# A layer norm with a spectral filter and an MLP: residual and bias on VectorE, W2 in SyncE's queue, the first square root on ScalarE, and a new order

## The chip, the cores and the metric

The kernel runs on one core of a Trainium2 chip. The metric is the device time of one execution in microseconds. Profiles are of one execution each; all times of instructions are counted from the start of its span.

## What is computed

```python
def reference(A_x, A_w_r, A_w_i, B_x, B_w1, B_b1, B_w2, B_b2):
    def _A_ref(x, w_r, w_i):              # x is (1, 2048, 640)
        X = rfft2(x.astype(float32)); X = X * (w_r + 1j * w_i)
        return irfft2(X, s=(S, D)).astype(bfloat16)
    def _B_ref(x, w1, b1, w2, b2):        # w1 is 640 x 1536, w2 is 1536 x 640
        h = gelu(einsum("bsd,df->bsf", x, w1) + b1)
        return einsum("bsf,fd->bsd", h, w2) + b2
    xn = _layernorm(A_x)                  # over the 640 columns, eps 1e-5
    return A_x + _A_ref(xn, A_w_r, A_w_i) + _B_ref(xn, B_w1, B_b1, B_w2, B_b2)
```

All inputs and the output are bf16.

## The kernel before

The 2048 rows are cut into 16 tiles of 128 rows, tile c holding the rows 16p + c. Both branches start from the same normalized tiles, and their results meet in PSUM.

**Normalization** (L574 to L603). For each tile VectorE takes statistics of two halves (`bn_stats`), aggregates them to mean and variance, adds eps (`ve`), GpSimd raises this to -1/2 (`rstd`, L580), VectorE forms `nmr = -mean * rstd` (L582) and then `x * rstd + nmr` (L603) into a buffer `xn`, of which there are two (for one pair of tiles each). Transposed tiles `xnT` come from PE (L619) with a copy by VectorE or ScalarE, or for the tiles in `BYDMA` from a DMA transpose that SyncE issues (L608).

**The spectral branch.** For each pair of tiles VectorE forms sums and differences (L632, L636), PE multiplies with the table `gtab` ("aps"), the result lies in `XV`. Then come six groups of products with `etab` (b0 to b5), evacuated to `Xb`; small 32 x 32 products with `mtab` (c00 to c31, first digit P of four steps, two each), evacuated to `Y`; the filter on VectorE, four products `T = Y * Wf` (L737) and four sums `Z` (L741) for each step P; small products with `ntab` (d00 to d31), evacuated to `U`; 16 DMA transposes of U into `XV` (L762); six groups with `getab`, evacuated to `Wf`, sums on VectorE (L788, L793), and last a product with `htab` into the output's PSUM.

**The MLP branch.** The W1 products ("hps") run in six blocks of 1, 1, 2, 4, 4 and 4 tiles, each for 12 pieces of 128 hidden columns; ScalarE applies Gelu (L670) into `gT`. The W2 products are 12 pairs of 512 and 128 columns for a tile. For tiles in `KEEP` they are done early and emptied to SBUF with b2 added (L839); for the others they are accumulated in the same PSUM as the `htab` product. VectorE's final add (L850) joins PSUM and the kept part, and SyncE stores the tile.

**Residual and b2.** For each tile there is an f32 place of 640 columns (`xo`), in `xnT` for tiles in `HOME`, else in `X`. It first holds b2 (a copy by ScalarE, L818) or the kept W2 result plus b2 (L839); then GpSimd issues a DMA that adds x from HBM to it (L841, accumulating). `QUIET` says for which transfers this DMA has to wait.

**What sets the order.** Every operation is given to `Sched` with an engine, a cost, a priority and its operands. `schedule` walks through time: of the operations that can start within 0.03 us of the earliest, the one with the highest priority is put next in its engine's queue; `sync` then places semaphore waits. So queues are fixed when the kernel is built, and an engine waits at an operation whose operands are late, with everything behind it. PSUM has eight banks, `ZONE` says which group may use which of them; `CHAIN` fixes the sequence of the b, c and d groups on PE, so that they alternate with MLP products. `WARM` gives the number of products on zeros with which PE starts (54, and 6 more behind the first transposes).

**Loads.** SyncE issues x, b1, most of W1, `gtab` and the 34 strided parts of the filter `Wf`, each with its own semaphore; ScalarE issues the identity and W1's first part; GpSimd issues `etab`, `mtab`, b2, W2 in four parts, `ntab`, `getab`, `htab`. W1 comes in parts of 2, 3 and 7 pieces of 128 columns.

Of the kernel before, what the change touches and what calls it, by code (L numbers as in the profile page):

```python
# [84 lines left out]

SWITCH = 0.095
HOLD = 0.04


def mm_us(n):  # L90
    return max(n / 2400.0 + 0.0027, 0.0265)
# [65 lines left out]
class Sched:  # L157
# [6 lines left out]
    def op(self, engs, prio, emit, reads=(), writes=(), after=(), nbytes=0, gate=(), rate=330e3, alts=None, late=0.0):  # L164
        o = Op()
        o.name = writes[0].name if writes else ""
        o.engs, o.prio, o.emit = engs, prio, emit
# [26 lines left out]
    def schedule(self):  # L194
# [24 lines left out]
        while left:  # L219
# [47 lines left out]
            if o.nbytes:  # L267
                if e == "pool":
                    dma_free = max(t + 2.0, dma_free) + o.nbytes / o.rate
                    o.end = max(t + 4.6, dma_free + 1.2)  # L270
                else:
                    s = max(t + 1.3, dma_free)
                    dma_free = s + o.nbytes / o.rate
                    o.end = dma_free + 0.35
            else:
                o.end = t + dur + LAT[e]
# [96 lines left out]
W1P = ((0, 2), (2, 5), (5, 12))  # L373
GROUPS = [(0, 2), (2, 3), (5, 3), (8, 3), (11, 3), (14, 2)]
BYDMA = (4, 8, 9, 10, 12, 14, 15)
WLATE = (17.0, 1.08)
ANY = [(0, 8)]
ZONE = {'hps': [(4, 8)], 'bps': [(0, 4)], 'cps': [(0, 4)], 'dps': [(0, 4)], 'eps': [(0, 4), (4, 8)], 'fin': [(4, 8), (0, 4)], 'fps': [(4, 8)], 'tps': [(0, 8)], 'aps': [(0, 8)]}
PRIO = {'hps': -60.2, 'gelu': -255.2, 'pb': 147.1, 'pc': 112.6, 'filt': 344.6, 'ipc': 182.7, 'eps': 72.7, 'fin': 71.9}
AHEAD = 1  # L380
EARLY = 4
CHAIN = "b0 b1 c00 c01 b2 c10 d01 c11 d00 b4 b3 c20 d10 c21 d11 b5 d20 d21 c30 c31 d31 d30".split()
XASPLIT = [((0, 1, 2, 3, 4),)] * 7 + [((0, 1), (2, 3, 4))]
KEEP = (0, 3, 5, 6, 7, 8, 11, 12, 14)
HOME = (0, 3, 1, 2, 4, 9, 10, 13)
QUIET = {0: 1, 3: 0, 6: 4, 9: 4, 12: 0, 15: 0, 1: 0, 2: 2, 4: 4, 5: 0, 7: 0, 8: 0, 10: 3, 11: 0, 13: 3, 14: 3}
WARM = (54, 6)
# [3 lines left out]
def bass_parallel_sum__spectral_gfnet__dense_activation_gelu__prompt_kernel(  # L391
# [21 lines left out]
    with ExitStack() as es:  # L413
# [22 lines left out]
        first = sb("first", [128, 1])  # L436
# [5 lines left out]
        nmr = sb("nmr", [128, 16], F32)  # L442
# [14 lines left out]
        XN, X1, XF = 0, 4 * D, 6 * D  # L457
# [7 lines left out]
        p_xn, p_x1, p_xf, p_xb, p_y, p_t, p_z, p_u = Pool(2), Pool(1), Pool(2), Pool(2), Pool(2), Pool(2), Pool(2), Pool(3)  # L465
# [25 lines left out]
        B_mh, B_xbpad, B_wpad, B_warm = Buf("mhalf"), Buf("xbpad"), Buf("wpad"), Buf("warm")  # L491
        K.op([("dve", 0.1)], 300, lambda e, _: e.memset(warm[:], 0.0), writes=[B_warm])
        K.op([("pool", 0.1)], 100, lambda e, _: e.memset(mhalf[:], -0.5), writes=[B_mh])
# [4 lines left out]
        K.op([("act", 1.45)], 300, lambda e, _: e.activation(first[:], warm[:, 0:1], ACT.Gelu_apprx_tanh), reads=[B_warm])  # L498
# [10 lines left out]
        B_g, B_e, B_m, B_n, B_ge, B_h, B_w2 = [Buf(x) for x in ("g", "e", "m", "n", "i", "h", "w2")]  # L509
# [15 lines left out]
        load_w1(1)  # L525
        load_x(2, 2)
        for j in range(2, len(W1P)):
            load_w1(j)
# [4 lines left out]
        for dst, src, buf, nbytes, rate, late in (  # L533
                (etab[:], const["E"], B_e, 204800, 250e3, 18.0), (mtab[:], const["M"], B_m, 65536, 130e3, 21.0),
                (b2bc[:], bass.AP(tensor=b2v.tensor, offset=b2v.offset, ap=[[0, 128], [1, D]]), B_b2b, 163840, 395e3, 22.0),
                *[(W2[:, 3 * j:3 * j + 3, :], w2v[:, 3 * j:3 * j + 3, :], B_w2, 3 * 128 * D * 2, 330e3, 24.0 + 4.0 * j) for j in range(4)],
                (ntab[:], const["N"], B_n, 49152, 130e3, 40.0), (getab[:], const["GE"], B_ge, 204800, 250e3, 50.0),
                (htab[:].rearrange("p a b -> p (a b)"), const["H"], B_h, 524288, 330e3, 55.0)):
            load(dst, src, buf, nbytes, rate=rate, q="pool", after=x_in, late=late)
        WP = 32 * KP  # L540
# [19 lines left out]
        pe([("128", 0.1)], 200, lambda: [(psb(B_b1ps.slot, [[1, NFC]]), b1t[:], ident[0:NFC, 0:NFC], True, True)], reads=[B_b1, B_id], writes=[B_b1ps])  # L560
        K.op([("act", 0.2)], 200, lambda e, _: e.activation(b1col[:], psb(B_b1ps.slot, [[1, NFC]]), ACT.Copy), reads=[B_b1ps], writes=[B_b1c])

# [5 lines left out]
        for c0, n in [(0, 1), (1, 1)] + [(c, 2) for c in range(2, 16, 2)]:  # L568
            pr = 100 - c0 / 2
            B_mv, B_ve, B_r = Buf("mv"), Buf("ve"), Buf("r")  # L570
            for c in range(c0, c0 + n):
                B_st = Buf("st")
                for h in range(2):
                    K.op([("dve", 0.393)], pr, lambda e, _, c=c, h=h: e.bn_stats(stats[:, c, 6 * h:6 * h + 6], view(X, c * D + H2 * h, [[1, H2]])),  # L574
                         reads=[B_x[c]], writes=[B_st], gate=first_ve if c == 1 else [])
                K.op([("dve", 0.119)], pr, lambda e, _, c=c: e.bn_aggr(mv[:, c, :], stats[:, c, :]), reads=[B_st], writes=[B_mv])
            a, b = c0, c0 + n
            o = K.op([("dve", 0.09)], pr, lambda e, _, a=a, b=b: e.tensor_scalar_add(ve[:, a:b], mv[:, a:b, 1], 1e-5), reads=[B_mv], writes=[B_ve])  # L578
            first_ve = first_ve or [o]
            K.op([("pool", 0.65)], pr, lambda e, _, a=a, b=b: e.tensor_tensor(out=rstd[:, a:b], in0=ve[:, a:b], in1=mhalf[:, a:b], op=ALU.pow),  # L580
                 reads=[B_ve, B_mh], writes=[B_r])
            K.op([("dve", 0.071)], pr, lambda e, _, a=a, b=b: e.scalar_tensor_tensor(out=nmr[:, a:b], in0=mv[:, a:b, 0], scalar=-1.0,  # L582
                                                                                     in1=rstd[:, a:b], op0=ALU.mult, op1=ALU.mult),
# [303 lines left out]
```

## Time and profile before

| | us |
|---|---|
| five runs, median (lowest to highest) | 152.91 (151.93 to 153.45) |
| the profiled execution | 151.77 |
| its span, first to last instruction | 149.6 |
| busy in the span: PE / VectorE / ScalarE / GpSimd | 143.1 / 110.7 / 79.5 / 33.0 |
| PE's first product on data, end of its last | 7.71, 147.19 |
| granted TensorE clock | 1.00 |

Busy time by stage (us), from the windows view:

| stage | from, to | PE | VectorE | ScalarE |
|---|---|---|---|---|
| head, until the first W1 product | 0, 7.71 | 6.47 | 3.27 | 2.16 |
| first tiles | 7.71, 13.69 | 5.82 | 5.91 | 5.11 |
| normalization, W1 blocks 0 to 2 | 13.69, 28.30 | 14.56 | 14.52 | 12.48 |
| normalization, W1 block 3 | 28.30, 46.70 | 18.29 | 16.26 | 15.79 |
| b0 to the first d group | 46.70, 62.83 | 15.35 | 10.71 | 7.56 |
| to the first getab group | 62.83, 110.95 | 46.85 | 28.96 | 29.63 |
| to PE's last product | 110.95, 147.19 | 35.71 | 30.76 | 6.74 |

How to read the profile's lines: an engine's line gives start, length, engine, line of the kernel, operation, out<-in with shapes, and in brackets how long the engine had been idle and who released it. A line of the waits view reads: engine and what it did, `<-` whom it waited for, us in total, times, the longest. A line of the groups view ends in busy us, the mean ns of one, and the idle time ahead of it. SPq, DVEq and so on are the engines' sequencers, which issue DMAs and process waits. Matmuls overlap in the records, so that lengths of single ones are longer than their distance; a few matmul records are missing.

### The profile page before, as it was taken

How to read it: one execution, taken by the hardware profiler on the slowest of the kernel's cores; microseconds unless marked ns; L12 is line 12 of the kernel's file. 1: busy time of each engine (PE TensorE's matmuls, PEld its weight loads, DVE VectorE, ACT ScalarE, POOL GpSimd, SP SyncE). 2: the span in 40 equal slices, each digit the busy share in tenths (PEclk: the TensorE clock that was granted, in tenths of full speed). 3: DMA queues.
4: the chain of work that ended last, by engine and by line, in shares of the span. 5: the costliest groups of instructions: out<-in, count | busy, mean ns of one | idle time of the engine just before them, and what ended most of it. 6: DMA issues, size and time to landing. Idle time of an engine off the chain costs nothing.

```text
span 149.6 us, 4118 instructions
## 1 busy us (share of the span) xinstructions
PE 143.1 (96%) x1720; PEld 89.4 (60%) x1743; DVE 110.7 (74%) x251; ACT 79.5 (53%) x137; POOL 33.0 (22%) x43
## 2 busy tenths in 40 slices
PE   7989999999999999899999999999999999999993
PEld 7989997554555646455533544344566666666563
DVE  1699999999974368969457955872009999999752
ACT  3189997777899335334798824767704024023000
POOL 1301252334220043320221026000398001000000
PEclk9999999999999999999999999999999999999999
DMA  4999468999996519492956457942799902622321
GB/s 131 351 395 397 139 125 179 225 171 262 238 210 131 123 44 164 156 176 49 106 117 92 88 105 144 202 83 42 104 166 221 243 21 88 196 75 86 131 86 46
DMA packets 33513, 22.84 MB, mean 153 GB/s; under 512 B 17336, under 2 KB 30776, under 8 KB 33496
## 3 DMA queue, kind: packets, MB, share of 16 engines
q1 hardware_dynamic: 25464, 13.81, 39.6%
q0 software_dynamic: 7232, 8.42, 28.7%
q10 hardware_dynamic: 800, 0.36, 0.8%
q8 instruction: 13, 0.21, 0.6%
q14 instruction: 4, 0.03, 0.1%
HBM read 13.58 MB, written 2.62 MB: 108 GB/s over the span
## 4 chain that ended last, share of the span: by engine, by line
PE 84%; DMA 5%; DVE 4%; issue 2%; SPq 1%; DVEq 1%
PE ps L474 83%; DMA W<-in_B_w_dram 5%; DVE T L737 2%; SPq L469 1%; PE ps L619 1%; DVE Z L741 1%; DVE Y L488 1%; DVEq L355 1%; DVE xnT L839 0%; DVE W L850 0%
## 5 line engine op out<-in xcount | busy, mean ns | idle before, releaser
L474 PE MATMUL ps<-W,gT 128*128 128x128 bf16 (+3 forms) x385 | 56.0, 293 | 1.2 <-issue 1.0
L474 PE MATMUL ps<-xnT,W 128*128 128x512 bf16 (+2 forms) x351 | 54.4, 306 | 1.4 <-issue 0.8
L474 PEld LDWEIGHTS ps<-W,gT 128*128 128x128 bf16 x396 | 29.8, 98 | 23.0 <-issue 1.9
L474 PEld LDWEIGHTS ps<-xnT,W 128*128 128x128 bf16 x360 | 28.9, 98 | 21.4 <-ACT gT L670 2.2
L670 ACT ACTIVATE gT<-ps,b1col 128x512 bf16<-128x512 f32 (+2 forms) x72 | 36.0, 557 | 7.7 <-PE ps L474 7.2
L841 POOL DMA_DIRECT2D xnT<-in_A_x_dram x8 | 13.0, 1815 | 36.4 <-ACT xnT L818 14.2
L487 ACT ACTIVATE Wf<-ps 128x960 bf16<-128x960 f32 (+1 forms) x8 | 6.7, 869 | 22.0 <-PE ps L474 22.0
L574 DVE BATCH_NORM_STATS2 stats<-X 128x6 f32<-128x320 bf16 x32 | 14.3, 472 | 2.2 <-DMA X<-in_A_x_dram 2.2
L841 POOL DMA_DIRECT2D X<-in_A_x_dram x8 | 8.9, 1111 | 29.0 <-DVE X L839 28.9
L737 DVE TENSOR_TENSOR T<-Y,Wf 128x1288 bf16<-128x1288 bf16 x16 | 12.4, 822 | 0.9 <-issue 0.8
L580 POOL TENSOR_TENSOR rstd<-ve,mhalf 128x2 f32<-128x2 f32 (+1 forms) x9 | 6.7, 742 | 27.2 <-DVE ve L578 27.2
L487 ACT ACTIVATE Xb<-ps 128x960 bf16<-128x960 f32 (+1 forms) x8 | 9.1, 1174 | 6.6 <-PE ps L474 6.4
L488 DVE CAST Wf<-ps 128x960 bf16<-128x960 f32 (+1 forms) x4 | 4.3, 1071 | 9.4 <-PE ps L474 9.2
L487 ACT ACTIVATE XV<-ps 128x1280 bf16<-128x1280 f32 (+1 forms) x8 | 9.5, 1185 | 2.3 <-PE ps L474 2.2
L488 DVE CAST Y<-ps 128x644 bf16<-128x644 f32 x8 | 6.6, 825 | 5.2 <-PE ps L474 5.2
L487 ACT ACTIVATE U<-ps 128x512 bf16<-128x512 f32 (+1 forms) x16 | 6.1, 434 | 6.5 <-PE ps L474 6.5
L487 ACT ACTIVATE Y<-ps 128x644 bf16<-128x644 f32 x8 | 5.7, 707 | 6.3 <-PE ps L474 6.3
L850 DVE TENSOR_TENSOR W<-ps,X 128x640 bf16<-128x640 f32 (+2 forms) x10 | 6.6, 686 | 3.0 <-PE ps L474 3.0
L636 DVE TENSOR_TENSOR T<-T 128x512 bf16<-128x512 bf16 (+1 forms) x32 | 8.6, 315 | 0.0
L488 DVE CAST Xb<-ps 128x640 bf16<-128x640 f32 (+1 forms) x4 | 4.3, 1065 | 5.6 <-PE ps L474 5.6
L474 PE MATMUL ps<-getab,XV 32*128 32x160 bf16 (+1 forms) x128 | 7.6, 242 | 0.0
L632 DVE TENSOR_TENSOR T<-T 128x640 bf16<-128x640 bf16 x16 | 7.2, 463 | 0.1
(55 smaller groups left out, 144.5 us busy)
## 6 DMA issues: line engine op xcount, KB each, us to landing
xnT<-in_A_x_dram POOLq DMA_DIRECT2D x8, 320.0 KB, 5.2
X<-in_A_x_dram POOLq DMA_DIRECT2D x8, 320.0 KB, 4.6
out_dram<-W SPq DMA_DIRECT2D x15, 160.0 KB, 1.8
X<-in_A_x_dram SPq DMA_DIRECT2D x7, 320.0 KB, 9.8
W<-in_B_w_dram POOLq DMA_DIRECT2D x4, 480.0 KB, 5.6
Wf<-in_A_w_r_dram SPq DMA_DIRECT2D x15, 80.2 KB, 5.0
Wf<-in_A_w_i_dram SPq DMA_DIRECT2D x15, 80.2 KB, 2.8
W<-in_B_w_dram SPq DMA_DIRECT2D x1, 1120.0 KB, 7.8
```

Of the source, the lines that this page charges most:

```text
L355: e.wait_ge(d.sem, d.count)
L474: ins = e.matmul(o_, lhsT=lw, rhs=rh, start=st, stop=sp_, skip_group_check=True)
L487: return e.activation(dst(), src(), ACT.Copy, scale=scale)
L488: return e.tensor_copy(dst(), src())
L574: K.op([("dve", 0.393)], pr, lambda e, _, c=c, h=h: e.bn_stats(stats[:, c, 6 * h:6 * h + 6], view(X, c * D + H2 * h, [[1, H2]])), reads=[B ...
L580: K.op([("pool", 0.65)], pr, lambda e, _, a=a, b=b: e.tensor_tensor(out=rstd[:, a:b], in0=ve[:, a:b], in1=mhalf[:, a:b], op=ALU.pow), read ...
L632: K.op([("dve", dve_us(640, 2))], pr, lambda e, _, k=k, op=op, xnv=xnv, x1v=x1v: e.tensor_tensor(out=x1v(H2 * k, [[D, 2], [1, H2]]), in0=x ...
L636: ring_ops.append(K.op([("dve", dve_us(4 * w, 2))], pr, lambda e, _, op=op, x1v=x1v, xfv=xfv, o_=o_, o0=o0, o1=o1, w=w: e.tensor_tensor(ou ...
L670: K.op([("act", act_us(128 * nt, 1))], pr + PRIO["gelu"], lambda e, _, c0=c0, nt=nt, fc=fc, hps=hps: e.activation(gT[:, fc, 128 * c0:128 * ...
L737: filt_ops.append(K.op([("dve", dve_us(4 * KP, 2))], pr, lambda e, _, k=k, Y=Y, TB=TB, pair=pair: e.tensor_tensor(out=view(TT, TB.slot * 8 ...
L841: K.op([("pool", 0.9 if c not in HOME else 1.5)], 51, lambda e, _, c=c, xov=xov, shaped=shaped: e.dma_start(xov(0, D), shaped(xv[:, c, :]) ...
L850: K.op([("dve", dve_us(w))], 95, lambda e, _, os_=os_, fps=fps, o0=o0, w=w, xov=xov, shaped=shaped, base=base: e.tensor_tensor(out=shaped( ...
```

## The change

The accumulating transfers, the ScalarE copies of b2, `HOME` and `QUIET` go. Instead VectorE adds x (from `X` in SBUF) and b2 into the tile's f32 place, at `RES` priority, and for kept tiles L839's successor adds PSUM to it. Even tiles have their place in `xnT`, odd ones in `X`. The `nmr` step goes: tiles are normalized as (x - mean) * rstd. For the first tile ScalarE takes the square root of variance + eps and VectorE the reciprocal; ScalarE therefore loads the table for Sqrt first and the one for Gelu behind it. `xn` has six buffers, four of them in `Y` and `Z`, so the first Y and Z, T wait for the DMA transposes. Tiles 11 and 13 join `BYDMA`. The W2 parts and `htab` are issued by SyncE, and each W2 part is waited for by itself. W1's parts are of 3, 4 and 5 pieces, and by its priority the second part is issued behind all x. b1's transposing product comes behind the first tile's transposes. PE starts with 46 products on zeros instead of 54. Seven tiles are kept instead of nine. The order on all engines is new: another `CHAIN`, other priorities, and a table `DELTA` of some 200 corrections to the priorities of single operations.

```diff
 SWITCH = 0.095
-HOLD = 0.04
+HOLD = 0.08
+DELTA = {'w1_1': -129.7, 'hps3_0': -215.2, 'hps5_11': -20.4, 'xe4': -26.5, 'hps3_1': -406.2,
...
-        o.engs, o.prio, o.emit = engs, prio, emit
+        o.engs, o.prio, o.emit = engs, prio + DELTA.get(o.name, 0.0), emit
...
-W1P = ((0, 2), (2, 5), (5, 12))
+W1P = ((0, 3), (3, 7), (7, 12))
-BYDMA = (4, 8, 9, 10, 12, 14, 15)
+BYDMA = (4, 8, 9, 10, 11, 12, 13, 14, 15)
...
-CHAIN = "b0 b1 c00 c01 b2 c10 d01 c11 d00 b4 b3 c20 d10 c21 d11 b5 d20 d21 c30 c31 d31 d30".split()
+CHAIN = "b0 b1 c01 c00 b2 c10 d00 d01 c11 b4 b3 c21 c20 d10 d11 b5 c31 d21 d20 c30 d30 d31".split()
-KEEP = (0, 3, 5, 6, 7, 8, 11, 12, 14)
+KEEP = (2, 3, 4, 5, 7, 8, 12)
+RES = 261.9
-WARM = (54, 6)
+WARM = (46, 6)
...
-        K.op([("act", 1.45)], 300, lambda e, _: e.activation(first[:], warm[:, 0:1], ACT.Gelu_apprx_tanh), reads=[B_warm])
+        K.op([("act", 1.45)], 300, lambda e, _: e.activation(first[:, 0:1], warm[:, 0:1], ACT.Sqrt), reads=[B_warm])
...
+        for j in range(4):
+            load(W2[:, 3 * j:3 * j + 3, :], w2v[:, 3 * j:3 * j + 3, :], B_w2[j], 3 * 128 * D * 2, rate=375e3, after=x_in, late=W2LATE[0] + W2LATE[1] * j)
...
+            if not c0:
+                o = K.op([("act", 0.2)], 300, lambda e, _: e.activation(ve[:, 0:1], mv[:, 0, 1:2], ACT.Sqrt, bias=epst[:]), reads=[B_mv, B_eps], writes=[B_ve])
+                K.op([("dve", 0.09)], 110, lambda e, _: e.reciprocal(rstd[:, 0:1], ve[:, 0:1]), reads=[B_ve], writes=[B_r])
+                K.op([("act", 1.45)], 300, lambda e, _: e.activation(first[:, 1:2], warm[:, 0:1], ACT.Gelu_apprx_tanh), reads=[B_warm], gate=[o])
...
-                    out=xnv(n, 0, [[1, D]]), in0=view(X, c * D, [[1, D]]), scalar1=rstd[:, c:c + 1], scalar2=nmr[:, c:c + 1], op0=ALU.mult, op1=ALU.add),
+                    out=xnv(n, 0, [[1, D]]), in0=view(X, c * D, [[1, D]]), scalar1=mv[:, c, 0:1], scalar2=rstd[:, c:c + 1], op0=ALU.subtract, op1=ALU.mult),
...
-                if not kept:
-                    K.op([("act", act_us(D))], 5, lambda e, _, xov=xov, shaped=shaped: e.activation(xov(0, D), shaped(b2bc[:]), ACT.Copy), reads=[B_b2b], writes=[xb2], after=free)
+                res_ops.append(K.op([("dve", 0.74)], RES - c / 10, lambda e, _, c=c, xov=xov, shaped=shaped: e.tensor_tensor(
+                    out=xov(0, D), in0=shaped(view(X, c * D, [[1, D]])), in1=shaped(b2bc[:]), op=ALU.add), reads=[B_b2b, B_x[c]], writes=[xb2 if kept else xo], after=free))
...
-                        out=xov(0, D), in0=shaped(psb(kps.slot, [[1, D]])), in1=shaped(b2bc[:]), op=ALU.add), reads=[kps, B_b2b], writes=[xb2], after=free))
-                K.op([("pool", 0.9 if c not in HOME else 1.5)], 51, lambda e, _, c=c, xov=xov, shaped=shaped: e.dma_start(xov(0, D), shaped(xv[:, c, :]), accum_op=ALU.add),
-                     reads=[xb2], writes=[xo], nbytes=327680, rate=164e3, after=quiet[QUIET[c]])
+                        out=xov(0, D), in0=shaped(psb(kps.slot, [[1, D]])), in1=xov(0, D), op=ALU.add), reads=[kps, xb2], writes=[xo]))
```

In the new queues PE has, from the end of the group c20 to the end of c30, 29 W1 products, b5 and 27 pairs of W2 products beside six small groups; VectorE has there twelve of the sixteen residual adds. SyncE issues tile 4's transpose, 13 parts of `Wf`, the transposes of 8 and 9, two parts, those of 10 and 11, those of 12 and 13, a W2 part and a small part of `Wf`, those of 14 and 15, a W2 part, 15 parts of `Wf`, the other W2 parts and `htab`.

## The prediction

> **What bounds the kernel now.** I read the page first, then who makes the matrix engine (PE) wait, then the timeline of the first 14 us, the chain around 62 us, and the VectorE groups by shape.
>
> ```profile
> PE 143.1 (96%) x1720; PEld 89.4 (60%) x1743; DVE 110.7 (74%) x251; ACT 79.5 (53%) x137; POOL 33.0 (22%) x43
> ...
> PE 84%; DMA 5%; DVE 4%; issue 2%; SPq 1%; DVEq 1%
> ```
>
> PE is busy 96% of the span and carries 84% of the chain that ended last. The list of PE's waits is short:
>
> ```profile
> PE ps L474 <- DVE Y L488: 0.4, 1, 0.4
> PE ps L474 <- ACT xnT L487: 0.2, 1, 0.2
> PE ps L474 <- DMA W<-in_B_w_dram: 0.2, 1, 0.2
> ```
>
> So from its first real product (7.71 us) to its last (147.19) PE is late by under 1 us. Time can be won only ahead of 7.71, by giving PE less work, or from the one 0.36 us stall at 62.8. It can be lost wherever the new order leaves PE without operands. The head, from the timeline (start, length):
>
> ```profile
> 0.99 5.64 PE L474 MATMUL ps<-warm 128*128 128x128 bf16 x54 [0.99 <-DVE warm L492]
> 1.70 1.28 ACT L498 ACT_TABLE_LOAD   x1 [1.70 <-PEq L872]
> ...
> 4.58 0.58 POOL L580 TENSOR_TENSOR rstd<-ve,mhalf 128x1 f32<-128x1 f32 x1 [3.47 <-DVE ve L578]
> ...
> 5.45 0.39 DVE L603 TENSOR_SCALAR T<-X,rstd,nmr 128x640 bf16<-128x640 bf16 x1
> ...
> 6.68 0.45 PE L619 MATMUL ps<-ident,T 128*128 128x128 bf16 x5
> ```
>
> The first tile is normalized at 5.45 us, but the 54 warm-up products hold PE until 6.57; its transposes start at 6.68. The stall, from the chain:
>
> ```profile
> 56.64 2.31 DVE T L737 x3
> 58.95 0.81 DVE Z L741 x2
> 59.76 0.74 DVE T L737
> 60.50 0.73 DVE xnT L839
> 61.23 0.81 DVE Z L741 x2
> 62.04 0.75 DVE Y L488
> 62.79 0.04 issue
> 62.83 1.38 PE ps L474 x36
> ```
>
> VectorE (DVE) filters two pairs in 4.7 us, has an unrelated add (L839) in between, empties one Y bank, and only then PE gets its inverse product.
>
> **Off the path.** The sixteen accumulating transfers (L841; 5.2 and 4.6 us from issue to landing) and ScalarE's seven bias copies (7 x 0.74 = 5.2 us) go. No PE wait in the list above names them, so removing them is worth nothing directly; their traffic could at most have stretched the landing of the XV transposes, which PE doesn't wait for at the first getab group (110.95 us), and a loss from taking them away has no place to come from. The W2 loads wait for no one either: in the new order their first use is near 80 us, SP issues the last by 52. They cost SP about 0.5 us each; two of them stand ahead of Wf loads, which the filter chain below counts.
>
> **PE work.** Tiles 11 and 13 are transposed by DMA: ten PE products of 56 ns less, **-0.56 us**. All other products stay. Tiles 2 and 4 now are "kept" and 0, 6, 11 and 14 are not; that moves products, it doesn't change their number.
>
> **The head.** The first tile's variance is known at 4.31 (the aggregate before the ve step); hand-over 0.09 (4.49 to 4.58 in the trace), a ScalarE operation of 0.20 (L498), hand-over, a reciprocal at the 0.15 of a 128x1 tensor_scalar: normalization starts at 4.85 instead of 5.45. Transposes need 0.61 more (7.56 to 8.17 in the second tile), so 5.45, but PE is still warming up. Here two rules speak against the change. The Trainium skill (TensorE: Matmul & The Clock Gate, "The HAM clock gate") lets a cold array take 107 ns for 128 columns until some 3.4 us of activity have passed; had that held from the first product at 0.99, 32 slow and 14 fast warm-ups (0.056) would end at 5.2, the transposes would run fast at 5.45, and the first real product would come near 6.8. The trace has 54 in 5.58 us, that is some 50 slow ones, the step at about 6.4. So 46 end at 0.99 + 46 x 0.107 = 5.90, still slow, and the five transposes run slow as well (+0.26). The other (ScalarE: Activation LUTs, "What ACT_TABLE_LOAD costs") prices every switch of the table at 1.28 us plus a drain of 1.38. The trace shows a load of 1.28 and the first ACTIVATE 0.02 behind it, with nothing ahead to drain. By the row, Gelu's table is back at 4.6 + 1.28 + 0.20 = 6.1 and hidden; by the rule 7.5, and the first product slips from 7.3 to 8.2, of which the idle time found next takes all but 0.3. I take the row. Evacuation: last transpose 6.33 + 0.21; b1's column is now copied ahead of it on ScalarE, so 6.77, and 0.54 later (7.17 to 7.71 before) the first real product: **7.31**, 0.4 earlier.
>
> That does not last. Tile 1's variance step stands behind the xnT copy on DVE (6.54), then three statistics of 0.40: its normalization starts at 8.1, transposes at 8.7 (before: 8.17). PE finishes its 15 products at 8.15 and idles 0.55. The next products read the W1 part with columns 7 to 11. Ahead of and with it 2.00 MB are queued, where before it was 2.66 MB, landed at 10.98; at 0.40 MB/us that is 9.35, a further 0.35 idle. From 9.4 on 35 products (1.96, tile 1's evacuation fits), then the first gtab group 0.56, tile 3's transposes until 12.6. Before, PE had at 13.69 done 73 such products, one gtab group and four transposes; the new order has the same at 12.58 + 23 x 0.056 = 13.87: **+0.2**.
>
> **13 to 45 us.** From tile 3's normalization (12.1 us) I add the rows in DVE's new order. DVE loses nine nmr steps (0.07 each in sequence) and three xnT copies (0.40), and normalizes the last tiles ahead of older pairs' sums, six buffers instead of two. Adding rows (statistics 0.40, aggregate 0.12, normalization 0.36, sums 0.37 and 0.95 per pair) I get tile 5's, 6's and 7's operands within 0.1 of when PE reaches them, pairs 3 to 7 ahead of PE: **+0.1**. Block 8 to 11 now rests on DMA transposes only. SP's sum: tile 4 at 17.15, five transposes of 1.28, fifteen Wf loads of 0.64, so tile 11 is issued at 31.9. Landing took 3.1 us (tiles 14, 15) to 5.5 (8, 9, between W2 loads that are no longer there): 35.0 to 37.4; PE wants it at 35.2. Nearer to the first: **+0.1**, at most 2.2.
>
> **Filter chain.** Y starts 0.15 behind c00, 34 waits of Wf loads take until 1.65 behind Y's start (54.98 to 56.64), then 4.6 for T and Z, 0.87 for Y: 7.3 us. PE has 5 and 12 and 5 products of 512, b2 and c10 between: 1.19 + 2.69 + 1.19 + 1.24 + 0.43 = 6.75. Stall 0.55 in place of 0.36: **+0.2**. The last Wf load is issued at 49.0 and lands at 52.1, before it is asked for at 54.0.
>
> **Residual adds.** Nearest rows:
>
> ```profile
> L632 DVE TENSOR_TENSOR T<-T 128x640 bf16<-128x640 bf16 x16 | 7.2, 463 | 0.1
> ...
> L839 DVE TENSOR_TENSOR X<-ps,b2bc 128x640 f32<-128x640 f32 x7 | 5.7, 820 | 1.4 <-PE ps L474 1.4
> ```
>
> The new add reads bf16 and writes f32. In sequence the rows stand 0.37 and 0.74 us apart. I take 0.74 because of the f32 output; 16 x 0.74 = 11.8 us more on DVE. Four lie between Xb and the Y of c20, twelve between the Y of c20 and of c30. From the end of c20 to the end of c30 PE has 29 W1 products of 512 or fewer columns (4.1 us), b5 (0.9), 27 pairs of W2 products of 512 + 128 (0.272 each, 7.3), and c31, c30, d10, d11, d21, d20 at about 0.6 with the change of array size (3.6): 15.9 us. DVE has Y 0.75, T 2.96, Z 1.62, two kept adds 1.5, twelve residuals 8.9: 15.7. It just fits. Then 21 pairs of W2 products (5.8) cover Y, T, Z (5.9): **+0.1**. At 0.37 each nothing changes on PE; each 0.08 above 0.74 costs 1 us.
>
> **Tail.** 30 pairs (8.1 us) stand between the last inverse product and the first getab group; before, landing took 7.1 from the last evacuation and that fits. Behind it DVE has 28 us in PE's 41: nothing.
>
> **Sum.** -0.56 + 0.2 + 0.1 + 0.1 + 0.2 + 0.1 = +0.1 us. The profiled execution took 151.77 (149.6 span and 2.17 around), so it would take 151.9; the median of the runs lies 1.14 above it, so **153.0 us**. Measurement can tell about 0.5%, 0.76 us, from no change.
>
> **Rivals.** (1) Even, as summed, 152.3 to 153.7: chance 0.38. (2) Faster: PE's early idle time (0.9) doesn't come, because W1 lands sooner than its bytes say or tile 1 is ready sooner, and the stall of 0.55 is covered by PE's small delays ahead of it. Then +0.1 - 0.9 - 0.5 = -1.3: 151.6. For it: two transposes less, no accumulating traffic near any load. Against: DVE's written order, variance behind the copy. Chance 0.35. (3) Slower: DVE becomes the bound between c20 and c30. Place: twelve residuals ahead of c30's Y. It decides from 0.76 us per add; at 0.87 (0.13 x 12) d30 waits 1.6 more: 154.7. For it: strided 5x128 writes and in-place sources have no row; against: L839 writes both shapes at 820 ns. Chance 0.27. That the new order isn't what runs can be excluded: the instruction lists show it.
>
> Range 151.3 to 154.7, from (2)'s price less a little to (3). Of (1), 0.31 lies within 0.5%, 0.03 below, 0.04 above; of (2) 0.32 is faster, of (3) 0.24 slower, the rest within: 0.35, 0.37, 0.28.
>
> **What would show it.** Right: first real product near 7.3, then PE gaps before tile 1's transposes and for W1; one PE wait near 0.5 at the first inverse product; residuals spaced 0.74; no PE wait at the first getab group. Wrong: PE waiting for an xnT transpose near 35 us by over 1 us, Gelu's table load followed by a long gap, residuals above 0.8, or PE waits at 100 us and later.

## The result, and the profile after

| | before | after |
|---|---|---|
| median of runs (lowest to highest), us | 152.90 (151.31 to 156.26), 79 runs | 152.73 (151.83 to 155.47), 44 runs |
| after / before, 95% interval | | 1.0014 (0.9998 to 1.0030) |
| the profiled execution, its span | 151.77, 149.6 | 153.11, 151.3 |
| PE's first product on data, end of its last | 7.71, 147.19 | 6.78, 148.95 |

The ratio leaves out the slow executions, those over 1.5% above the fastest of their kernel, of which the kernel before has more (18 of 79, against 1 of 44); so it is not the quotient of the two medians. Nothing has changed that this measurement can tell: 0.2 us more by the ratio, 0.2 us less by the medians. The two profiled executions differ by 1.34 us, though. That of the kernel before was among its fastest (nine of its 79 runs took less, and a quarter lie below 152.2), that of the changed kernel among the upper half of its own (152.46 to 153.0 hold the middle half). This will matter below.

The page of the changed kernel, the line of busy times and that of the chain:

```profile
PE 141.3 (93%) x1701; PEld 87.2 (58%) x1725; DVE 114.2 (75%) x244; ACT 80.8 (53%) x143; POOL 9.3 (6%) x22
...
PE 74%; DMA 8%; ACT 5%; DVE 4%; SPq 4%; issue 3%
```

PE is busy 1.8 us less (eight products on zeros and ten transposing ones are gone, and the rest of those on zeros went by faster) in a span that is 1.7 us longer, so it idles 3.5 us more. DMA comes up in the chain that ended last. PE's waits in the changed kernel (whom it waited for, total, times, longest):

```profile
PE ps L483 <- issue: 2.7, 11, 1.1
PE ps L483 <- DMA W<-in_B_w_dram: 1.9, 2, 1.1
...
PE ps L635 <- DVE Z L617: 0.4, 1, 0.4
PE ps L483 <- DVE xnT L856: 0.3, 1, 0.3
PE ps L483 <- ACT xnT L496: 0.3, 1, 0.3
PE ps L483 <- ACT T L496: 0.3, 1, 0.3
```

Three waits are large: two for parts of W1, and one put down to "issue" that is 1.1 us long. Where they are, from the timeline of PE (start, length, in brackets the idle time ahead):

```profile
0.99 4.08 PE L483 MATMUL ps<-warm 128*128 128x128 bf16 x46 [0.99 <-DVE warm L501]
5.50 0.45 PE L635 MATMUL ps<-ident,Z 128*128 128x128 bf16 x5 [0.42 <-DVE Z L617]
...
6.78 1.01 PE L483 MATMUL ps<-xnT,W 128*128 128x128 bf16 x15 [0.28 <-ACT xnT L496]
9.51 2.13 PE L483 MATMUL ps<-xnT,W 128*128 128x128 bf16 x35 [1.12 <-DMA W<-in_B_w_dram]
...
19.31 3.08 PE L483 MATMUL ps<-xnT,W 128*128 128x256 bf16 x38 [0.79 <-DMA W<-in_B_w_dram]
...
60.64 0.51 PE L483 MATMUL ps<-Z,ntab 32*32 32x320 bf16 x32 [1.10 <-issue]
```

The first real product comes 0.93 us earlier than before. Then PE waits: 1.12 us at 9.51 for W1's pieces 7 to 11, 0.79 at 19.31 for its pieces 3 to 6 (issued at 7.03 behind all x, 12.1 us to landing), and 1.10 at the first inverse product, where the kernel before waits 0.36. What held that product, from VectorE's timeline, first of the kernel before, then of the changed one:

```profile
54.98 0.83 DVE L488 CAST Y<-ps 128x644 bf16<-128x644 f32 x1 [1.10 <-PE ps L474]
56.64 2.31 DVE L737 TENSOR_TENSOR T<-Y,Wf 128x1288 bf16<-128x1288 bf16 x3 [0.83 <-issue]
```

```profile
53.01 0.83 DVE L497 CAST Y<-ps 128x644 bf16<-128x644 f32 x1 [0.78 <-PE ps L483]
55.01 2.31 DVE L756 TENSOR_TENSOR T<-Y,Wf 128x1288 bf16<-128x1288 bf16 x3 [1.17 <-DMA Wf<-in_A_w_i_dram]
```

Y starts two microseconds earlier than before (53.01, 54.98), but the last filter load is issued at nearly the same time (51.3, 51.6). So the filter products (T) now wait for the landing of that load: T starts 2.00 behind Y, not 1.66.

### The profile page after: what moved, and what is told of

Same layout as the page of the kernel before. It is cut to its first block, busy times and chain, and to the rows that moved or that the text cites. A ratio compares the mean times of both kernels' runs of the same rounds, so it can differ in the third digit from the quotient of the medians.

```text
span 151.3 us, 4055 instructions
## 1 busy us (share of the span) xinstructions
PE 141.3 (93%) x1701; PEld 87.2 (58%) x1725; DVE 114.2 (75%) x244; ACT 80.8 (53%) x143; POOL 9.3 (6%) x22
## 4 chain that ended last, share of the span: by engine, by line
PE 74%; DMA 8%; ACT 5%; DVE 4%; SPq 4%; issue 3%
PE ps L483 74%; DMA W<-in_B_w_dram 8%; SPq L478 4%; DVE T L756 2%; ACT gT L688 1%; DVE Z L760 1%; ACT T L496 1%; ACT U L496 1%; ACT XV L496 1%; DVE Y L497 1%; DVE xnT L856 0%; ACT Y L496 0%; ACT xnT L496 0%; DVE W L865 0%
## 5 line engine op out<-in xcount | busy, mean ns | idle before, releaser
L483 PE MATMUL ps<-W,gT 128*128 128x512 bf16 (+3 forms) x384 | 54.5, 293 | 1.3 <-issue 0.6
L496 ACT ACTIVATE Xb<-ps 128x960 bf16<-128x960 f32 (+1 forms) x9 | 9.8, 1137 | 2.8 <-PE ps L483 2.6
L811 DVE TENSOR_TENSOR Wf<-Wf 128x960 bf16<-128x960 bf16 (+1 forms) x12 | 6.7, 598 | 5.7 <-PE ps L483 5.5
L496 ACT ACTIVATE U<-ps 128x512 bf16<-128x512 f32 (+1 forms) x14 | 5.4, 447 | 8.0 <-PE ps L483 8.0
L496 ACT ACTIVATE Y<-ps 128x644 bf16<-128x644 f32 x10 | 6.9, 711 | 3.1 <-PE ps L483 3.1
L865 DVE TENSOR_TENSOR W<-ps,xnT 128x640 bf16<-128x640 f32 x8 | 6.5, 818 | 1.9 <-PE ps L483 1.9
L597 POOL TENSOR_TENSOR rstd<-ve,mhalf 128x2 f32<-128x2 f32 (+1 forms) x8 | 5.9, 737 | 27.4 <-DVE ve L596 27.4
L806 DVE TENSOR_TENSOR Wf<-Wf 128x960 bf16<-128x960 bf16 (+1 forms) x12 | 6.9, 597 | 0.9 <-ACT Wf L496 0.7
L483 PE MATMUL ps<-etab,XV 32*128 32x160 bf16 (+1 forms) x128 | 7.2, 232 | 0.3 <-ACT T L496 0.3
L497 DVE CAST Y<-ps 128x644 bf16<-128x644 f32 x6 | 5.0, 827 | 3.2 <-PE ps L483 3.2
L483 PEld LDWEIGHTS ps<-etab,XV 32*128 32x128 bf16 (+1 forms) x128 | 5.5, 95 | 3.1 <-ACT T L496 0.8
## 6 DMA issues: line engine op xcount, KB each, us to landing
W<-in_B_w_dram SPq DMA_DIRECT2D x1, 640.0 KB, 12.1
```

Of the source, the lines that this page charges most:

```text
L483: ins = e.matmul(o_, lhsT=lw, rhs=rh, start=st, stop=sp_, skip_group_check=True)
L496: return e.activation(dst(), src(), ACT.Copy, scale=scale)
L497: return e.tensor_copy(dst(), src())
L806: K.op([("dve", dve_us(320 * n, 2))], pr + 2, lambda e, _, k=k, op=op, yo=yo, y2=y2, n=n: e.tensor_tensor(out=view(Wf, Y2 + y2.slot * 3 * ...
L811: K.op([("dve", dve_us(320 * n, 2))], pr + 3, lambda e, _, k=k, op=op, y2=y2, yf=yf, n=n: e.tensor_tensor(out=view(Wf, YF + yf.slot * 3 * ...
L865: K.op([("dve", dve_us(w))], 95, lambda e, _, os_=os_, fps=fps, o0=o0, w=w, xov=xov, shaped=shaped, base=base: e.tensor_tensor(out=shaped( ...
```

## The experiments

Two theories at the start. **M**: PE bounds the kernel; what the change wins (a shorter head, two transposes less) is spent in the three PE waits; the accumulating transfers, and the VectorE additions that replace them, are both worth nothing. **R1**: the transfers cost the kernel before about 1 us; the change won it and VectorE's additions gave it back. All ratios are to the kernel before, run beside. Code is shown in extracts, with `...` where lines are left out.

### Without the transfers, without the additions, with more additions

The kernel before, transfers taken out of GpSimd's queue:

```diff
+gone = {o for o in K.order["pool"] if o.nbytes == 327680}
...
+K.order["pool"] = [o for o in K.order["pool"] if o not in gone]
```

> The kernel before without its sixteen accumulating transfers, everything else in the same order. It leaves out the residual x, nothing else. Theory M (the engine that bounds is PE, and the transfers were off its path): no change, within 0.3% of the kernel before, and PE's waits the same three short ones. Rival R1 (the transfers cost the kernel before about 1 us, which the change won and gave back on VectorE): 0.6% or more faster, some 1 us, to be seen as PE idle time that is gone. Should the transfers be what spreads the times of the kernel before, the spread of its runs (1.0 us) falls towards the 0.5 us of the kernel after.

Measured: 0.9955 (0.9933 to 0.9978), 0.7 us faster. That is between the theories: M's zero is wrong, R1's place for it is open. The spread falls, as the expectation's last sentence has it: the middle half of the runs spans 0.7 us, that of the kernel before beside it 1.1. The profiled execution doesn't show the gain; it took 153.38, far above the median of 151.73, and most of its excess lies behind PE's last product (PE ends at 147.55 of a span of 151.6; in the kernel before at 147.19 of 149.6). The chain of the kernel before, its pieces behind the head and at the end (start, length, what):

```profile
13.85 5.49 PE ps L474 x77
...
137.42 9.78 PE ps L474 x84
```

and of the kernel without transfers:

```profile
14.19 5.50 PE ps L474 x77
...
137.77 9.78 PE ps L474 x84
```

123.57 and 123.58 us lie between: in these two executions the transfers cost PE nothing there. So the gain must come from executions that these profiles are no example of, or from outside this stretch.

The changed kernel without the additions:

```diff
+gone = set(res_ops)
...
+K.order["dve"] = [o for o in K.order["dve"] if o not in gone]
```

> The changed kernel without the sixteen VectorE additions of x and b2 (about 12 us of VectorE). It leaves out the residual and b2 (the f32 places of the tiles that are not kept hold what was there). Theory M: VectorE just fits between the groups c20 and c30, so taking the additions away brings at most the two waits of 0.3 us that PE has behind them: 0 to 0.4% faster than the changed kernel, that is 152.1 to 152.8 us. Rival R1 (the additions gave back about 1 us that the removed transfers had won): 0.7% or more faster, below 151.7 us.

Measured: 1.0038 (1.0017 to 1.0060), no faster than the changed kernel. VectorE is busy 102.7 us instead of 114.2, and from the first inverse product to the end of PE's last there are 88.32 us (60.38 to 148.70), with the additions 88.31. The additions cost 0.0 us. R1's second half falls.

The changed kernel, additions of even tiles doubled:

```diff
+for o in res_ops[0::2]:
+    p = _copy.copy(o)
...
+    dve.insert(dve.index(o) + 1, p)
```

> The changed kernel with the additions of the eight even tiles done twice (the second writes the same values), six of the eight between c20 and c30, at 0.735 us each: 4.4 us more VectorE work in that stretch. Theory M (VectorE is exactly full there, break-even near 0.76 us per addition): the last d groups wait some 4 us longer, 156 to 157.5 us, and nearly all of it in one or two PE waits at d30 and c30. If VectorE had room in that stretch (the rival that my sum of the stretch is too tight): under 1 us slower, below 153.8 us.

Measured: 1.0429 (1.0383 to 1.0475), 158.96 us. VectorE was full, as M says; but 6.2 us are more than 4. Its timeline shows PE waiting 1.29 us (for Y, which two doubled additions ahead of it delay) and 2.16 (for the other six):

```profile
77.73 0.52 PE L483 MATMUL ps<-Z,ntab 32*32 32x320 bf16 x32 [1.29 <-DVE Y L497]
...
97.75 5.11 PE L483 MATMUL ps<-W,gT 128*128 128x512 bf16 x24 [2.16 <-DVE X L856]
```

Behind the second wait the granted clock falls. The stretches of 1 us from 98, columns: stretch, length, busy time (and instructions) of PE, PEld, DVE, ACT, POOL, then the clock, DMA share, GB/s:

```profile
98.00:99.00 1.00, 1.00 (x9) 0.59 (x8) 1.00 (x2) 0.00 (x0) 0.00 (x0) 1.00 0.00 0
99.00:100.00 1.00, 1.00 (x6) 0.52 (x4) 1.00 (x3) 0.00 (x0) 0.00 (x0) 0.52 0.00 0
100.00:101.00 1.00, 1.00 (x5) 0.52 (x4) 1.00 (x2) 0.00 (x0) 0.00 (x0) 0.50 0.00 0
101.00:102.00 1.00, 1.00 (x5) 0.51 (x4) 1.00 (x3) 0.00 (x0) 0.00 (x0) 0.50 0.00 0
102.00:103.00 1.00, 0.86 (x5) 0.25 (x3) 1.00 (x4) 0.00 (x0) 0.00 (x0) 0.78 0.00 0
```

The missing shares (0.48 + 0.50 + 0.50 + 0.22) are 1.7 us of PE work. At 60.8 us this profile is only 0.12 behind that of the changed kernel, at PE's end 6.25. The two waits, the 1.7 us and three short waits (0.21 at 91.6, 0.20 at 103.1, and 0.16 more at 104.0) make 5.7 of these 6.1 us.

### The kernel before, once more

> The kernel before once more, unchanged: a second profile of it and a comparison of equals. If its spread (1 us) comes from when the granted TensorE clock of the first microseconds steps up (6.4 us in the profile shown, near 5.5 in the run without accumulating transfers) the first real product lies at 7.0 to 7.7 and the rest of the trace is the same, so the end of PE moves with it. If it comes from the accumulating transfers: PE waits behind 14 us that the first profile does not have. Ratio 1.000 within its interval.

Measured: 0.9980 (0.9947 to 1.0013), as it should be. The profiled execution took 153.15 us, and PE ends 1.57 later than in the first profile. Its timeline of PE, the lines with a wait that the first one lacks:

```profile
9.52 1.57 PE L474 MATMUL ps<-xnT,W 128*128 128x128 bf16 x25 [0.30 <-DVE xnT L488]
11.50 1.44 PE L474 MATMUL ps<-xnT,W 128*128 128x128 bf16 x23 [0.40 <-ACT gT L670]
15.54 2.94 PE L474 MATMUL ps<-xnT,W 128*128 128x128 bf16 x40 [0.32 <-DVE xnT L488]
...
112.48 1.07 PE L474 MATMUL ps<-getab,XV 128*128 128x160 bf16 x16 [0.58 <-DMA XV<-T]
```

Both halves of the expectation were half right. The head: the first product is at 7.37 instead of 7.71, but by the transposes at 13.80 (13.41 in the first profile) it is 0.4 behind, and once the wait at 15.54 is over 0.8; from that wait the chain leads back to the landing of x. That is half of the 1.57, and the run without transfers has two of these three waits too (0.64 at 9.48, 0.42 at 11.47). And at the first getab group PE waits 0.58 us for transposes of U into XV. From the chain:

```profile
106.07 2.28 SPq L762
108.36 0.04 issue
108.40 4.03 DMA XV<-T
```

The last transpose landed 4.03 us behind its issue, in the first profile 3.0, without transfers 3.3. That could be the accumulating transfers, which were moving data from 109 us on. But the transpose before it held SyncE for 2.28 us, where it took 1.28 in the other two, and until 108 us no accumulating transfer was moving: that microsecond has another cause, which is open, and by these numbers PE would not have waited without it (0.58 is less than 1.0). Earlier, landings are longer with the transfers: the two transposes from `gtab`'s buffer at 93 us took 5.8 (mean) in the first profile, 6.6 in this one, 4.0 without transfers; PE doesn't wait for them. So the transfers cost 0.7 us (0.3 to 1.0) by the run without them; where PE loses it is not shown.

A part of it lies outside of what the profiles show. The time of an execution is longer than the span of its instructions. In all 206 executions of the changed kernel and of its edits the difference is 1.74 to 1.87 us. In the kernel before, run beside them, it is over 2.5 in 25 of 181 executions, and up to 3.76; without transfers it is at most 2.12 (22 executions). Of the 0.7 us, about 0.2 is this difference (2.04 and 1.86, means), the rest is in the span.

### W1's parts

The part with pieces 3 to 6 (`w1b`) ahead of the last two x:

```diff
...
+sp.remove(w1b)
+sp.insert(sp.index([o for o in sp if o.name == "x8"][0]), w1b)
```

> The changed kernel, but SyncE issues the W1 part with pieces 3 to 6 two places earlier, ahead of the last two x loads. Theory M (PE idles 0.8 us at 19.3 because this part, issued at 7.03 behind all x, lands at 19.2): it lands near 17.5, that wait is gone, PE ends 0.4 to 0.8 us earlier, ratio to the changed kernel 0.995 to 0.997, about 152.0 us. Rival (VectorE's normalization of the last tiles sets the pace there, and the later x make it later still): the wait at 19.3 turns into waits for transposed tiles of the same size, no change, 152.7 us or a little more.

Measured: 1.0005 (0.9978 to 1.0032), 152.54 us; the expected 0.995 to 0.997 of the changed kernel is neither shown nor excluded. The trace has the wait at 19.3 gone and PE's end at 148.30, 0.65 earlier. All four runs with this edit (this one and three combinations below) lack that wait. But it isn't there in every execution without it either: the profiles without additions, with one flag and with W1 in two loads have it (1.07, 0.96, 1.28), those with doubled additions and with only W2 parts moved don't. In the run here 0.30 came back as a wait for a transposed tile at 34.9, and the stall at the first inverse product grew from 1.10 to 1.34, since PE got there earlier and the filter's landing didn't follow as far.

The part with pieces 7 to 11 in two loads:

```diff
...
+wa.emit = lambda e, _: e.dma_start(view(W1, 128 * 10, [[F, 5], [1, 256]]), w1v[:, :, 1280:1536])
+wb.emit = lambda e, _: e.dma_start(view(W1, 128 * 7, [[F, 5], [1, 384]]), w1v[:, :, 896:1280])
```

> The changed kernel, but the W1 part with pieces 7 to 11 is loaded by two DMAs, pieces 10 and 11 (which PE uses first) ahead of 7 to 9. Theory M (behind the first tile PE waits 0.3 to 1.1 us at 9.2 to 9.5 for this part's landing): the wait is cut by at least half. But the next wait, at 19.3, is for a landing that this does not move, so PE idles that much longer there: end to end under 0.3 us, 152.5 to 152.9 us. Rival (the head's gain goes through to the end once the wait at 9.5 is gone): 0.5 us or more faster, below 152.2 us.

Measured: 1.0050 (1.0024 to 1.0075), 153.13 us. PE's wait near 9.5 fell to 0.30, now for a transposed tile, and the next one, at 19.53, grew to 1.28 for W1, as M says. That it is slower than the changed kernel (by 0.4 us) was not expected; in its profile the filter's products start at 55.85, 0.84 later than in the changed kernel, though SyncE issued the loads only 0.15 later. Why they landed so late is open. So the landing can slip by 0.8 us from one execution to another with no load moved.

### The filter's loads and its waits

GpSimd waits for the loads, VectorE for one flag:

```diff
+one = K.op([("pool", 0.1)], 0, lambda e, _: e.memset(flag[:], 0.0), writes=[Buf("flag")])
+one.deps, one.eng, one.start = list(B_w.writers), "pool", 1e3
...
+    o.deps = [d for d in o.deps if d not in B_w.writers] + [one]
```

> The changed kernel, but the 34 semaphores of the filter's loads are waited for by GpSimd, which is idle then and sets one flag; VectorE's first filter product waits for this flag alone. Theory M (34 waits at some 0.05 to 0.1 us each on VectorE's queue lengthen the way from the first Y to the first T, 2.0 us in the profile, and this stands in the 1.1 us stall of PE at the first inverse product): T starts 0.7 to 1.3 us earlier, the stall falls to 0.4 us or less, the time falls by 0.5 to 1.1 us. Rival (the last filter load lands late, it is the landing that is waited for): the start of T moves by under 0.3 us and the time by nothing.

Measured: 1.0010 (0.9981 to 1.0038), no change, as the rival has it. The flag itself was set late, so it was the landing:

```profile
54.76 0.10 POOL L873 MEMSET flag<- 128x1 f32 x1 [17.64 <-DMA Wf<-in_A_w_i_dram]
```

> The changed kernel, but the first two W2 parts are issued behind the last load of the filter instead of in the middle of them. Both theories of the stall at 60.6 (1.1 us; 0.78 in the run without residuals) have a part: the last filter load lands near 54.7, and VectorE's waits, one after another, are done 1.66 us behind the start of Y, also at 54.7. With the loads earlier by some 1 us only the landing goes: the first T moves from 55.0 to 54.7, the stall to 0.78, PE ends 0.3 us earlier, about 152.4 us. If the landing alone held it: T near 53.9, the stall at most 0.3, 151.9 us. If the waits alone held it: no change.

The edit did something else than this expectation says. The W2 parts are not queued in the order of their numbers; it moved one part closer to the filter's last fifteen loads and put another ahead of them. SyncE's queue from 36.7 us on:

```diff
-W2, Wf, xnT x2, W2, Wf x15, W2 x2, htab
+Wf, xnT x2, W2 x3, Wf x15, W2, htab
```

Measured: 1.0133 (1.0079 to 1.0187), six executions. The filter products start at 56.04, 3.4 behind Y, and PE's stall is 2.52. One W2 part more ahead of the loads: the last is issued 0.7 us later, and they land one microsecond later. A dose that I hadn't meant to give, but the time follows it.

> The changed kernel with four edits: the W1 part of pieces 3 to 6 ahead of the last two x, the part of 7 to 11 in two DMAs, the first two W2 parts behind the filter's last load, and one flag by GpSimd in place of VectorE's 34 waits. Theory M (what the change won, a shorter head and two transposes less, is spent in three PE waits: 0.3 to 1.1 at 9.4, 0.8 at 19.3, 1.1 at 60.6): most of all three goes, T starts 0.9 us behind Y and the stall at 60.6 is 0.2 or less; 1.4 to 2.2 us faster than the changed kernel, 150.5 to 151.3 us, ratio to the kernel before 0.985 to 0.992. Rival (the waits are only where other limits show, VectorE's pace up to 45 us and from 70 to 91 us takes back what is gained): under 0.8 us faster, 152 us or more.

Here that edit, W1's two and the flag were made together. Measured: 1.0157 (1.0076 to 1.0238), 156.0 us in six executions, far on the rival's side. The three W2 parts again: the flag at 56.10, a stall of 2.38 us, and behind it the granted clock at 0.50 to 0.74 from 63 to 67 us (1.7 us).

The edit that was meant, in the same stretch of the queue:

```diff
-W2, Wf, xnT x2, W2, Wf x15, W2 x2, htab
+Wf, xnT x2, Wf x15, W2 x4, htab
```

> The changed kernel, with all four W2 parts behind the last filter load in SyncE's queue (the run named e7_a_w2_late did not do this: the parts are not queued in the order of their numbers, and it put three parts ahead of the last fifteen filter loads instead of two). Theory S (the last filter loads are late because SyncE issues them late: two W2 parts ahead of them took 1.63 and 0.58 us of its time, and with three the landing slipped from 54.9 to 56.0): the last filter load is issued 2 us earlier and lands near 52.7, the first T then starts 1.66 us behind Y as VectorE's waits allow, near 54.7 instead of 55.0 to 55.1, the stall is 0.8: 0.2 to 0.5 us faster than the changed kernel, about 152.3 us. Rival (DMA traffic decides, not issue: four parts and htab right behind the filter loads slow their last packets): landing no earlier than 54.5, no gain.

Measured: 1.0013 (0.9991 to 1.0035), 152.60 us. The last load is issued at 50.0 and lands 2.5 later, T starts 1.68 behind Y and the stall is 0.78, as theory S says: now it is VectorE's waits, not the landing. The run without additions, in which no load was moved, has the same (1.67, 0.78), so the step from 1.10 to 0.78 is within what one execution differs from another. Nothing is gained over all; the profile has a wait of 0.71 at 36.1 for a transposed tile.

> The changed kernel with three edits: W1's pieces 3 to 6 ahead of the last two x, all W2 parts behind the last filter load, and one flag by GpSimd in place of VectorE's waits. Theory S: the landing (52.7) and the waits (1.66 behind Y) both go, the first T starts within 1 us of Y, the stall at the first inverse product falls from 1.1 to 0.3 us or less; with the 0.8 us wait at 19.3 gone: 1.2 to 1.9 us faster than the changed kernel, 150.8 to 151.6 us, ratio to the kernel before 0.986 to 0.993. Rival (the loads land late whatever is ahead of them in the queue): stall above 1 us, 152.3 us or more.

Measured: 0.9974 (0.9951 to 0.9998), 152.16 us. A gain over the kernel before is not shown by this: in the same session the kernel before, compared with itself, gave 0.9980. The run with the W2 parts alone, also of that session, took 152.60, so the other two edits are worth 0.4 us by the medians. That is far from the 1.2 to 1.9 expected, and the stall is still 0.84, so S was too hopeful: the last load was issued at 49.6 and the flag set at 53.81, 4.2 us later. In the run with the W2 parts alone, with the same parts behind it in the queue, the last load took 2.5; why it took longer here is open.

To these three edits, one more in SyncE's queue behind the last x:

```diff
-Wf x3, xnT (tile 4), Wf x13, xnT x2
+Wf x8, xnT (tile 4), Wf x8, xnT x2
```

> As the run with three edits (W1's pieces 3 to 6 ahead of the last two x, W2 parts behind the filter loads, one flag), and besides five more filter loads go ahead of tile 4's transpose, for which SyncE stands still from 11.2 to 16.3 us. Theory S (the first inverse product still waits 0.84 us there because the last filter load, issued at 50.2, lands at 53.8): SyncE is done with the filter about 3 us earlier, the landing comes ahead of Y (52.2), the first T starts within 0.95 us of Y's start, the stall falls to 0.1 us or less: 0.6 to 0.9 us faster than with three edits, 151.2 to 151.6 us, ratio to the kernel before 0.990 to 0.995. Rival (the early loads take DMA time from x and W1, or tile 4's and later transposes land later): the stall goes but waits of 0.5 us or more come at 15 to 36 us, 152 us or more.

Measured: 0.9987 (0.9960 to 1.0015), 152.19 us. S and its rival both hold: the flag is set at 50.64, T follows Y at once, and the stall is gone:

```profile
52.42 0.83 DVE L497 CAST Y<-ps 128x644 bf16<-128x644 f32 x1 [0.78 <-PE ps L483]
53.23 2.31 DVE L756 TENSOR_TENSOR T<-Y,Wf 128x1288 bf16<-128x1288 bf16 x3
```

In exchange PE waits 0.60 us for tile 4's transpose at 24.5, and its runs spread from 151.26 to 153.43. The profiled execution (151.51) beats the three edits, the median doesn't. The stall in numbers:

| kernel | last filter load issued | Y | first T | T behind Y | PE's stall |
|---|---|---|---|---|---|
| before | 51.6 | 54.98 | 56.64 | 1.66 | 0.36 |
| changed | 51.3 | 53.01 | 55.01 | 2.00 | 1.10 |
| without additions | 51.0 | 53.07 | 54.74 | 1.67 | 0.78 |
| doubled additions | 50.6 | 52.70 | 55.13 | 2.43 | 1.47 |
| W1 part early | 51.0 | 52.11 | 54.35 | 2.24 | 1.34 |
| W1 part in two loads | 51.4 | 53.21 | 55.85 | 2.64 | 1.67 |
| one flag | 50.9 | 53.01 | 54.89 | 1.88 | 0.98 |
| three W2 parts ahead | 52.0 | 52.63 | 56.04 | 3.41 | 2.52 |
| no W2 part ahead | 50.0 | 53.30 | 54.98 | 1.68 | 0.78 |
| three edits | 49.6 | 52.20 | 53.94 | 1.74 | 0.84 |
| and filter early | 48.0 | 52.42 | 53.23 | 0.81 | none |

Each row is one execution. With the filter's loads where the change put them the stall is anything from 0.78 to 1.67, by when the last load happens to land; the run with a third W2 part ahead of them (2.52) lies outside that range, and so does the last row. Two limits lie nearly on top of each other, VectorE's waits (1.66 to 1.68 behind Y) and the landing. Taking either away alone shows no gain in time; taking both away brings T to 0.81 behind Y instead of 1.68. That this shortens the kernel is not shown either.

## Why the prediction was right, and where not

The even outcome and the median came as forecast (153.0, measured 152.73), though even had a chance of 0.35 and faster 0.37. The sum behind it did not all hold. Compared profile with profile, the step was +1.34 us and not +0.1; the medians agree because an error on the other side cancels it, and that is luck.

- **Head.** The steps were right in their place and their result: 73 products, a gtab group and four transposes were predicted done at 13.87 and were done at 13.88 (12.59 + 23 x 0.056; 13.61 in the run without additions). The way there depends on the execution. In the run without additions, in which the faster pace of products came late, the transposes began at 5.87 and the first real product at 7.27 (predicted 5.90 and 7.31); in the changed kernel's own profile the pace changed near 3.9 us (46 products in 4.08 us are some 27 of 107 ns and 19 of 56), and the product at 6.78. In both W1's pieces 7 to 11 let PE go on only at 9.2 to 9.5. So the head's gain was spent there, as said. The table load took the row's 1.28 us (4.78 to 6.06) and the next ScalarE operation began at 6.07: the row was the right choice against the rule's drain.
- **13 to 45 us**, the first step that failed. DMA transposes at 35 us cost nothing, as one end had it. But PE waits 0.79 us at 19.31 for W1's pieces 3 to 6. The prediction worked out when the part of pieces 7 to 11 lands and not this one, although it had been moved behind all x. By its sum the filter was asked for at 54.0, so Y at 52.35; Y came at 53.01. Three other profiles with the part in this place have the wait (0.96 to 1.28), three don't; in those PE waits 0.2 to 0.7 at 35 us for a transposed tile instead, so that this limit lies close behind.
- **Filter chain**: right mechanism, wrong size. The stall was put at 0.55 from a filter chain limited by VectorE's waits; it is 0.78 where these limit it and 1.10 in the changed kernel's profile. "The last Wf load is issued at 49.0 and lands at 52.1, before it is asked for at 54.0" is the failing sentence: it was issued at 51.3 and landed just ahead of 55.0. SyncE's sum was 2.3 us short: two W2 parts took 2.2 us instead of 1.0, thirteen loads behind tile 4's transpose 0.71 each instead of 0.64.
- **Residual adds**: right. They are 0.735 us apart (0.74 taken), the twelve just fit, and without them not one PE wait goes away. That they also have no slack, the doubled ones show. This is the answer to rival (3); rival (2) falls because both of its conditions failed, PE's early idle time and the stall came, and (1) is what was seen.
- **"Removing them is worth nothing directly"** for the accumulating transfers: wrong, by 0.7 us (0.3 to 1.0). The argument was that PE waits for none of them in the profile. The profile was one execution, and what an execution takes beyond its span, in some up to 3.76 us, is in no wait of PE. In the second profile PE does wait 0.58 at the first getab group; that the transfers caused it is not shown. (The list of PE's waits from which the argument starts also leaves out the line `issue`, 1.7 us in eleven pauses of at most 0.2. The changed kernel has them too, so the comparison stands.)
- **Median over profile.** The sum added the 1.14 us by which the runs lie above the profiled execution as if it belonged to both kernels. For the changed kernel it is -0.38. The second profile of the kernel before shows of what kind such a difference is, 0.8 us lost by waits in the first 16 us and 0.6 at the first getab group; which of them the change removes was not tested.

Where the gain went, then, in four terms (the first compares many runs, the second is a count, the last two are waits of single executions): -0.7 for the transfers, -0.56 for two transposes (counted, not isolated), +0.79 for W1's part, +0.74 for the stall at the first inverse product (1.10 - 0.36), together +0.3 us; the ratio says +0.2. The agreement proves little, since both waits differ by several tenths from execution to execution. What the head and two PE waits of 0.3 us (at 80.8 and 97.8, there without additions too) add or take is of the same size and was not separated. Of the theories, M holds for VectorE's additions and for the waits, R1 for the transfers; neither was whole.

## What to carry over

One profile is one execution: before a cost is set to nothing because nobody waits for it there, see whether the profile is a fast one of a wide spread, and take a second. When a change pulls a chain forward or moves loads behind others in one queue, work out for each load when it is issued (sum the queue, with every DMA in it) and when it is now asked for; here W1's part had been moved back, and the filter's loads stayed where they were while the work that needs them came 2 us forward. Where two limits end within 0.3 us of each other, removing one can gain no more than that. And when an edit makes a wait in a profile go away, see whether the wait comes in every execution without the edit.

## What was not expected of the hardware

The step to a faster pace in the head is not a property of the kernel: the same 54 products took 5.64, 5.30 and (without the transfers) 4.79 us, the same 46 products 4.08 to 5.09. It is read from the products alone: between 3 and 4 us PE starts 9 or 10 of them, between 4 and 5 us 9 in the kernel before, 14 without the transfers and 16 in the changed kernel. The profile's column of the granted clock says 1.00 throughout the head, so that the clock is the likely cause but not a shown one. The Trainium skill (TensorE: Matmul & The Clock Gate, "The HAM clock gate") speaks of it in the section that the prediction used: the window in which activity is counted runs freely, so the step differs from run to run. The prediction took one trace's 6.4 us for fixed.

PE waits of 2.16 us (doubled additions) and 2.38 us (all four edits) were followed by about 3.5 us at half the clock, 1.7 us of work each; one of 2.52 us was not. The same section names an idle window of about 3.4 us for the clock to fall; here less idle time sufficed in two traces of three. There a stall of a little over 2 us cost nearly twice its length (2.16 and 1.7).
